# Leftover tokens of all batches in shared transfers, the guard's number in PSUM, the general path as a loop, and a new order of the work

## The chip, the cores and the metric

The kernel runs on one core of a Trainium2 chip. The metric is the device time of one execution in microseconds (us). Engines are named as the profile names them: PE (matrix products), PEld (weight loads of PE), DVE (vector), ACT (activation), POOL (GpSimd), SP (the engine whose queue issues every DMA of this kernel).

## The reference

Four batches of 12,480 tokens with 128 channels, 32 inducing vectors, and two weight matrices of a layer with 2,048 hidden units, all float32:

```python
def mab(q, kv):
    s = scale * (q @ kv.transpose(0, 2, 1))
    s = s - s.max(-1, keepdims=True)
    a = np.exp(s)
    a /= a.sum(-1, keepdims=True) + 1e-09
    return a @ kv
h = mab(I, x)              # 32 rows for each batch, from all its tokens
x = mab(x, h)              # every token, from those 32 rows
y = x @ w_in
g = y - np.tanh(y)
out = g @ w_out            # 49,920 x 128
```

## The kernel before

The kernel does not run the layer on 49,920 tokens. Every token's attention output is a mix of 32 rows of `h`, and these rows lie close together. So it expands `y - tanh(y)` around the mean row of each batch, carries the 32 rows through both weight matrices once for each batch (`linear`), and gets a 32 x 128 matrix `P`. An output token is then its 32 weights times `P`, divided by the sum of its weights. A guard (`bound`) works out how large the error of the expansion can be, against rounding and against the smallest sum of weights, and writes one number, `limit`. At the end all engines load `limit` and branch (L846, L847): if it is above zero, a general path computes the layer in full, token by token (`general`). With the inputs of this case the general path is not taken.

A batch is cut into 8 segments of 1,536 tokens and a rest of 192 (`NS`, `LEFT`), so there are nine steps for each batch, 36 in all. Each step occurs in two phases.

- `first(b)`: a segment is loaded with channels on the partitions (`xT`, L380), scored against the inducing vectors (`scores`, L357), copied to SBUF with its running maximum on DVE (L391). When the maxima of a group of segments are met, ACT takes the exponential (L461), DVE transposes blocks (L465), and PE accumulates the weighted sum of the tokens (L472). For that the tokens are needed with tokens on the partitions: 16 of the 32 segments are loaded a second time in that layout (`xn`, L455), the other 16 (`TURNED`) are transposed by PE (L447) and copied by ACT or DVE (L451).
- `second(b, s)`: the same `xT` tile is scored against `h` (L357 again), DVE finds a maximum (L625, L626), ACT takes the exponential (L629), PE multiplies by `P` (L636). DVE collects the sums of weights into `S_all` (L648) and takes reciprocals (L651). Each of the four quarters of a segment is then normalised in one of two ways: by DVE in one step (L660), or copied by ACT (L664) and multiplied by POOL (L669). The result is stored by SP (L695).

The rest of 192 tokens goes through the same steps with smaller tiles: `xr` (channels first, 98 KB, L380), `xnr` (tokens first, 98 KB, L455) and `otr` (output, 98 KB, L695), one transfer each for each batch, twelve in all. In SBUF `xr` has three places, `xnr` and `otr` two; scores of the rest stand on partitions 0 to 63.

Weights come in as 64-bit words (`weight`) and are turned into float32 by ACT, POOL and DVE over the first third of the span.

The order of the work is written out ahead by a planner in the program (`Plan.order`), not found at run time. Each operation is put in with an engine, an estimated cost, what it reads and writes, and a priority. The planner walks in simulated time over its own costs; whenever an engine is free it takes, of the ready operations, the one with the lowest priority number, with an added `STAY` for a change of PE mode. It also limits how many large buffers may hold tiles of a kind at one time (`MOST`). Priorities are built from the table `K`, one number for each kind of operation and batch; `DVQ` says how many quarters of a segment go to DVE at first, `GROUPS` where the maxima are met. Every engine then runs its list in that order, waiting on semaphores. SP's list holds all loads and stores, so a store whose data is not ready holds back what is behind it.

The guard's last steps run behind everything: `smin` is the minimum of all 432 columns of `S_all` (L750), PE turns it and two other columns into rows (L754 to L756), and `decide` makes `limit` on DVE in ten instructions (L763 to L771, with a scratch row `low` in SBUF):

```python
v.tensor_tensor(out=x[:, 3:4], in0=x[:, 3:4], in1=x[:, 3:4], op=ALU.mult)
v.tensor_tensor(out=x[:, 3:4], in0=x[:, 3:4], in1=x[:, 0:1], op=ALU.subtract)
v.tensor_scalar(out=limit, in0=x[:, 3:4], scalar1=0.0, scalar2=None, op0=ALU.max)
```

Of the kernel before, what the change touches and what calls it, by code (L numbers as in the profile page):

```python
# [26 lines left out]
SWITCH, STAY = 0.115, 73.1  # L27
MOST = dict(xT=15, xn=16, ot=61, pm=9)
K = dict(load=(-405.2, -73.6, 365.6, 732.0), step1=(189.5, 37.3, 86.1, 34.3), lag2=(-1344.7, 642.2, -187.9, 554.4),
         copy=(-966.7, 182.8, 582.0, 890.5), step2=(63.0, 5.9, 46.9, 4.9), turn=(3399.7, 2729.3, 3806.6, 3390.1), move=(-926.9,  # L30
         616.0, 643.2, -1883.0), nat=(445.7, -196.7, -60.7, 77.0), exp1=(-409.6, -1802.6, 1772.8, 577.3), et=(-1268.2, -670.6,
         821.4, -2142.2), acc=(63.5, 1115.9, -997.2, -2667.1), sc2=(498.0, -379.7, -952.9, 693.2), top=(984.0, 131.6, 1260.3,
         -21.4), exp2=(1257.9, -709.0, 2777.2, -857.8), prod=(-1778.1, 1760.3, -578.0, -21.4), rec=(-2172.0, -394.3, 355.7,
         404.0), ev=(2492.2, -544.6, -1227.1, -3030.9), off=(-545.7, 642.1, 1621.1, 2136.7), step3=(173.1, 138.3, 60.8, 306.6),
         st=(-962.2, -256.6, 745.9, -225.9), norm=(-114.8, 1199.2, -943.7, -185.5), lw1=-186.8, lw2=25.2, w1=74.7, w2=591.6,
         bound=2765.6)
# [3 lines left out]
LOADED = [(b, s) for b in range(4) for s in range(8) if s not in TURNED[b]]  # L40
WMIN = 1.125 * 2.0 ** -15
# [152 lines left out]
def fused_kernel(ctx, tc, xT, xn, xl, indT, w_in, w_out, out):  # L194
    nc = tc.nc
    C, NTOK = xT.shape
    B = xl.shape[0]
# [36 lines left out]
    PLACES = dict(big=23, xr=3, xnr=2, s1=11, et=3, ex=3, otr=2, mb=4, ps=8, W=1)  # L234
# [38 lines left out]
    sums_all = small("S_all", [128, B * COLS], 1)  # L273
# [85 lines left out]
    xT_b = {}  # L359

# [6 lines left out]
    def first(b, pri):  # L367
# [8 lines left out]
        for s in range(NSG):  # L376
            nq, sg, kb = shape(s)
            base = b * N + s * SG
            x = xT_b[b, s] = big("xT", [C, SG]) if s < NS else io_buf("xr", [C, LEFT])
            add("SP", 2.0 if s < NS else 0.35, lambda x=x, base=base, n=nq * sg: nc.sync.dma_start(out=x.get(), in_=xT[:, base:base + n]),  # L380
                writes=[x], pri=pri + s + K["load"][b])
            ps = misc()
            s1 = io_buf("s1", [128, SEG])
            add("PE", 0.645 if s < NS else 0.18, lambda x=x, ps=ps, nq=nq, sg=sg: scores(ps.get(), x.get(), nq, sg, indT_sb, True),
                reads=[x, ind_b, s1], writes=[ps], pri=pri + K["step1"][b] * s, mode="c")
            s1s.append(s1)
            part = Buf()
            mx_parts.append(part)

            def copy(ps=ps, s1=s1, s=s, P=nq * m, sg=sg):  # L390
                nc.vector.tensor_scalar(out=s1.get()[:P, :sg], in0=ps.get()[:P, :sg], scalar1=1.0, scalar2=None,  # L391
                                        op0=ALU.mult, op1=ALU.max, accum_out=mxg.get()[:P, s:s + 1])
            add("DVE", 0.52 if s < NS else 0.28, copy, reads=[ps, mxg], writes=[s1, part], pri=pri + K["step1"][b] * s + K["copy"][b])

# [34 lines left out]
        for s in range(NSG):  # L429
            nq, sg, kb = shape(s)  # L430
            P = nq * m
            g0 = group[s]
            q0 = p + K["step1"][b] * cut[g0 + 1] + K["step2"][b] * (s - cut[g0])
            if s < NS:
                x = big("xn", [128, KB, C])
            else:
                x = io_buf("xnr", [QL * 32, KL, C])
# [16 lines left out]
            else:  # L454
                add("SP", 2.0 if s < NS else 0.3, lambda x=x, s=s: nc.sync.dma_start(  # L455
                    out=x.get(), in_=xn[LOADED.index((b, s))] if s < NS else xl[b]), reads=[xT_b[b, s]], writes=[x], pri=q0 + K["nat"][b])
# [155 lines left out]
    def second(b, s, pri):  # L612
# [8 lines left out]
        add("PE", 0.645 if full else 0.18, lambda: scores(ps.get(), x.get(), nq, sg, hT_all[:, b, m:], True),  # L621
# [31 lines left out]
        ot = big("ot", [128, NQ * R, C]) if full else io_buf("otr", [SEGL, QL, C])  # L653
        pieces = []

        def slot(q0, q1):
            return ot.get()[:T, q0 * nr:q1 * nr, :]
# [34 lines left out]
        at = b * N + s * SG  # L692
        dst = out[at:at + nq * sg, :].rearrange("(p k) c -> p k c", p=T)
        for q0, q1 in ((0, 2), (2, 4)) if late and full else ((0, nq),):
            add("SP", (2.12 if full else 0.35) * (q1 - q0) / nq, lambda q0=q0, q1=q1: nc.sync.dma_start(  # L695
                out=dst[:, q0 * nr:q1 * nr, :], in_=slot(q0, q1)), reads=[ot, *pieces[q0:q1]], pri=pri + K["st"][b])


    def bound(pri):
# [41 lines left out]
        def least():  # L741
# [7 lines left out]
        smin, low = small("smin", [128, 1], 1), small("low", [1, 4], 1)  # L749
        add("DVE", 0.5, lambda: nc.vector.tensor_reduce(out=smin.get(), in_=sums_all.get(), axis=AX.X, op=ALU.min),  # L750
            reads=[sums_all, *s_parts], writes=[smin], pri=pri)

        def turn():
            nc.tensor.transpose(out=ps3.get()[:1, :B], in_=r1.get(), identity=ident[:B, :B])  # L754
            nc.tensor.transpose(out=ps3.get()[:1, 128:256], in_=r2.get(), identity=ident)
            nc.tensor.transpose(out=ps3.get()[:1, 256:384], in_=smin.get(), identity=ident)  # L756
        add("PE", 0.5, turn, reads=[r1, r2, smin, ident_b], writes=[ps3], pri=pri, mode="f")

        def decide():

            v = nc.vector
            x = low.get()
            v.tensor_reduce(out=x[:, 0:2], in_=ps3.get()[:1, 128:384].rearrange("o (k p) -> o k p", k=2), axis=AX.X, op=ALU.min)  # L763
            v.tensor_reduce(out=x[:, 2:3], in_=ps3.get()[:1, :B], axis=AX.X, op=ALU.min)
            v.tensor_tensor(out=x[:, 0:1], in0=x[:, 0:1], in1=x[:, 2:3], op=ALU.min)
            v.reciprocal(out=x[:, 2:3], in_=x[:, 1:2])
            v.tensor_scalar(out=x[:, 3:4], in0=x[:, 1:2], scalar1=-2.0, scalar2=2.0 * (m + SLACK), op0=ALU.mult, op1=ALU.add)
# [142 lines left out]
```

## Time and profile before

| | |
|---|---|
| Median of 3 runs | 187.9 us (186.53, 187.91, 187.90) |
| Profiled execution, its own time | 189.09 us |
| Its span, first to last instruction | 187.2 us |
| Busy: PE, PEld | 154.7 us (83%), 99.5 us (53%) |
| Busy: DVE, ACT, POOL | 149.6 (80%), 112.7 (60%), 95.5 (51%) |
| DMA | 68.84 MB, mean 368 GB/s |
| Mean granted clock of PE | 0.957 |

The profile is one execution on the chip. Busy time counts instructions that work, not those that wait, branch or issue transfers. An entry `L669 POOL TENSOR_TENSOR big<-big,mb 128x384` is line 669 of the kernel, engine, operation, written tile, read tiles, and partitions by elements. A table of stages has, after the length, the busy time of PE, PEld, DVE, ACT and POOL with the number of instructions in brackets, the granted PE clock as a share of full speed, the mean busy share of the 16 DMA engines, and the GB/s that they moved. A name with a q behind the engine (SPq) is the engine's sequencer, which waits, branches and issues transfers. A row of waits reads: who waited for whom, microseconds in total, times, longest. A row of one line's instructions has shortest, median and longest duration in ns and the first and last start in us. The chain of waits is the work that ended last, followed back from the end. The queue q1 carries the kernel's own transfers, q8 and q14 carry program code.

### The profile page before, as it was taken

What the parts mean: (1) busy time and instruction counts of PE and PEld (TensorE: products, weight loads), DVE (VectorE), ACT (ScalarE), POOL (GpSimd) and SP (SyncE); (2) the same over time, 40 slices, a digit from 0 to 9 for tenths busy, and PEclk for the clock granted to TensorE, in tenths of its full rate; (3) what the DMA queues carried; (4) which work ended last, traced back from release to release, by engine and by line L of the source; (5) the groups of instructions that cost most, each with busy time, mean ns of one, the idle gap of its engine ahead of it and who ended that gap; (6) DMA issues with size and microseconds to landing.
All of it is one profiled execution on the core that took longest, in us unless ns stands there. A gap on an engine that the chain in (4) does not pass through costs nothing.

```text
span 187.2 us, 7373 instructions
## 1 busy us (share of the span) xinstructions
PE 154.7 (83%) x2895; PEld 99.5 (53%) x2895; DVE 149.6 (80%) x574; ACT 112.7 (60%) x282; POOL 95.5 (51%) x114
## 2 busy tenths in 40 slices
PE   0799966879988999999999978999979988879500
PEld 0465554645345865565667864556556764646300
DVE  3268699999999987896889863599899879998950
ACT  3022389964168974756779953438589574578600
POOL 5000124672250368456755583460675886499960
PEclk9999999999999999999999995799999999999955
DMA  5999998999999999999999999699989999999991
GB/s 144 406 423 415 404 409 253 393 420 422 414 419 367 295 326 312 375 423 416 404 356 363 383 420 422 211 416 347 364 314 382 418 417 415 404 421 390 387 390 50
DMA packets 14489, 68.84 MB, mean 368 GB/s; under 512 B 1776, under 2 KB 2928, under 8 KB 14448
## 3 DMA queue, kind: packets, MB, share of 16 engines
q1 hardware_dynamic: 14448, 68.31, 94.2%
q8 instruction: 24, 0.39, 0.8%
q14 instruction: 17, 0.14, 0.2%
HBM read 42.75 MB, written 25.56 MB: 365 GB/s over the span
## 4 chain that ended last, share of the span: by engine, by line
PE 55%; DVE 20%; ACT 7%; DMA 6%; issue 5%; POOL 3%; SPq 0%; DVEq 0%; ACTq 0%; POOLq 0%
PE ps L357 17%; PE ps L636 13%; PE ps L447 10%; PE ps L472 9%; DMA big<-in_xn 3%; ACT s L461 3%; PE ps L353 3%; DMA big<-in_xT 2%; POOL big L669 2%; DVE s L391 2%; PE ps L527 2%; DVE mb L625 2%; DVE ps L327 2%; DVE big L320 2%; ACT big L323 1%
## 5 line engine op out<-in xcount | busy, mean ns | idle before, releaser
L669 POOL TENSOR_TENSOR big<-big,mb 128x384 f32<-128x384 f32 (+1 forms) x73 | 75.2, 1056 | 46.2 <-ACT big L664 41.9
L664 ACT COPY big<-ps 128x384 f32<-128x384 f32 x99 | 41.1, 488 | 8.2 <-DVE S_all L648 7.7
L636 PE MATMUL ps<-P_all,ex 32*128 32x129 f32 (+1 forms) x784 | 36.0, 294 | 4.1 <-issue 1.5
L636 PEld LDWEIGHTS ps<-P_all,ex 32*128 32x128 f32 (+1 forms) x784 | 28.1, 188 | 19.6 <-ACT big L664 5.2
L357 PE MATMUL ps<-big,indT_sb 128*32 128x384 f32 x256 | 28.1, 516 | 6.4 <-DMA big<-in_xT 6.0
L451 ACT COPY big<-ps 128x512 f32<-128x512 f32 x30 | 17.0, 587 | 25.8 <-PE ps L447 24.5
L472 PE MATMUL ps<-big,et 128*32 128x128 f32 x768 | 27.3, 275 | 5.8 <-DVE et L465 4.1
L629 ACT ACTIVATE ex<-ps,mb 128x384 f32<-128x384 f32 (+1 forms) x36 | 19.7, 553 | 17.8 <-DVE mb L626 10.8
L447 PEld LDWEIGHTS ps<-ident,big 128*128 128x128 f32 x192 | 21.6, 146 | 13.2 <-issue 4.9
L447 PE MATMUL ps<-ident,big 128*128 128x128 f32 x192 | 27.9, 290 | 0.9 <-DVE win_sb L329 0.9
L357 PE MATMUL ps<-big,hT_all 128*32 128x384 f32 x256 | 27.6, 502 | 0.2 <-DVE s L391 0.2
L472 PEld LDWEIGHTS ps<-big,et 128*32 128x32 f32 x768 | 21.0, 110 | 11.3 <-DVE et L465 5.0
L391 DVE TENSOR_SCALAR_CACHE_REDUCE s<-ps 128x384 f32<-128x384 f32 (+1 forms) x36 | 18.1, 513 | 8.8 <-PE ps L357 7.8
L461 ACT ACTIVATE s<-s,nbs 128x384 f32<-128x384 f32 (+1 forms) x36 | 21.0, 586 | 0.5 <-DVE nbs L412 0.5
L625 DVE TENSOR_REDUCE mb<-ps 128x1 f32<-128x384 f32 (+1 forms) x36 | 18.4, 511 | 2.6 <-PE ps L357 2.2
L648 DVE TENSOR_SCALAR S_all<-ps 128x3 f32<-128x3 f32 (+1 forms) x136 | 13.5, 153 | 7.3 <-PE ps L636 6.4
L465 DVE STREAM_TRANSPOSE et<-s 128x384 f32<-128x384 f32 (+1 forms) x36 | 18.1, 519 | 0.3
L660 DVE TENSOR_TENSOR big<-ps,mb 128x384 f32<-128x384 f32 x29 | 15.5, 544 | 0.3
L314 POOL TENSOR_SCALAR big<-big 128x512 f32<-128x512 f32 x8 | 5.4, 683 | 20.0 <-DMA big<-in_w_in 20.0
L451 DVE COPY big<-ps 128x512 f32<-128x512 f32 x18 | 12.3, 687 | 2.4 <-PE ps L447 2.2
L357 PEld LDWEIGHTS ps<-big,indT_sb 128*32 128x32 f32 x256 | 6.9, 113 | 12.0 <-issue 8.8
L357 PEld LDWEIGHTS ps<-big,hT_all 128*32 128x32 f32 x256 | 8.0, 111 | 5.1 <-issue 2.6
(118 smaller groups left out, 158.4 us busy)
## 6 DMA issues: line engine op xcount, KB each, us to landing
big<-in_xT SPq DMA_DIRECT2D x32, 768.0 KB, 8.8
out<-big SPq DMA_DIRECT2D x30, 768.0 KB, 7.6
big<-in_xn SPq DMA_DIRECT2D x16, 768.0 KB, 6.9
big<-in_w_in SPq DMA_DIRECT2D x4, 512.0 KB, 12.8
big<-in_w_out SPq DMA_DIRECT2D x4, 512.0 KB, 8.2
out<-big SPq DMA_DIRECT2D x4, 384.0 KB, 4.9
xr<-in_xT SPq DMA_DIRECT2D x4, 96.0 KB, 10.5
xnr<-in_xl SPq DMA_DIRECT2D x4, 96.0 KB, 7.0
```

The costliest lines, as they stand in the source:

```text
L357: nc.tensor.matmul(ps[q * m:(q + 1) * m, :sg], lhsT=w, rhs=seg(x, nq, None, q), start=True, stop=stop)
L391: nc.vector.tensor_scalar(out=s1.get()[:P, :sg], in0=ps.get()[:P, :sg], scalar1=1.0, scalar2=None, op0=ALU.mult, op1=ALU.max, accum_out=mx ...
L447: nc.tensor.transpose(out=ps.get()[:, k * 128:(k + 1) * 128], in_=xt.get()[:, c:c + 128], identity=ident)
L451: copy(x.get()[:, 4 * g:4 * g + 4, :].rearrange("p k c -> p (k c)"), ps.get())
L461: nc.scalar.activation(out=t, in_=t, func=AF.Exp, bias=nbs.get()[:P, g:g + 1], accum_out=sums.get()[:P, s:s + 1])
L465: add("DVE", 0.5 if s < NS else 0.25, lambda et=et, s1=s1s[s], P=P, sg=sg, kb=kb: nc.vector.transpose(out=et.get()[:P, :kb].rearrange("p k ...
L472: nc.tensor.matmul(hacc.get()[q * m:(q + 1) * m, g * C:(g + 1) * C], lhsT=et.get()[:P, k, :], rhs=x.get()[:P, k, :], start=first_k[g, q] = ...
L625: nc.vector.tensor_reduce(out=mb.get()[:P, 0:1], in_=ps.get()[:P, :sg], axis=AX.X, op=ALU.max)
L629: add("ACT", 0.49 if full else 0.28, lambda: nc.scalar.activation(out=ex.get()[:P, :sg], in_=ps.get()[:P, :sg], func=AF.Exp, bias=mb.get() ...
L636: nc.tensor.matmul(o_b[q].get()[:T, r * (C + 1):(r + 1) * (C + 1)], lhsT=ex.get()[p, r * T:(r + 1) * T], rhs=P_all[p, b, :], start=True, s ...
L664: nc.scalar.copy(out=slot(q, q + 1), in_=o(q)[:, :, :C])
L669: nc.gpsimd.tensor_tensor(out=x, in0=x, in1=mb.get()[:T, 2 + q0 * nr:2 + q1 * nr].unsqueeze(2).to_broadcast([T, w, C]), op=ALU.mult)
```

## The change

1. The rests of all four batches are loaded by two transfers: `xr` (128 partitions x 3,072 bytes) for the channels-first layout, and `xl` for the other one, where batches 0 and 2 lie on partitions 0 to 63 and batches 1 and 3 on 64 to 127. Both are issued with batch 0. Scores of the rest of odd batches therefore stand on partitions 64 to 127 (`at`). Rests get scratch tiles of their own (`s1r`, two places; `s1` has ten places in place of eleven).
2. The rests are stored by two transfers: batches 0 to 2 together once batch 2's rest is normalised, then batch 3.
3. The guard takes the minimum of `S_all` in two parts: all columns but those of the last three steps first (an early instruction), then the last 36 columns and the early result. Two of the three turns and their reductions (`room`) move ahead of the last step. What is left (`decide`) is five instructions on a scratch row in PSUM, with a formula that needs no reciprocal.
4. In the general path the loop over the 16 blocks of hidden units becomes a loop of the program (`tc.For_i`) in place of 16 copies of its body; partial outputs are added by DVE in SBUF and no longer accumulated in PSUM.
5. `K`, `STAY`, `MOST`, `TURNED`, `GROUPS` and `DVQ` have new values. 16 segments are turned and 16 loaded twice, as before.

```diff
-SWITCH, STAY = 0.115, 73.1
-MOST = dict(xT=15, xn=16, ot=61, pm=9)
+SWITCH, STAY = 0.115, 31.6
+MOST = dict(xT=15, xn=12, ot=48, pm=7)
 ...
-TURNED = ((0, 1, 2, 3, 4, 5, 6, 7), (1, 2, 6), (1, 2, 4, 7), (0,))
-GROUPS = ((0,), (0,), (0,), (0, 3))
-DVQ = ((2, 1, 1, 1, 2, 3, 2, 0, 1), (2, 1, 0, 2, 1, 3, 1, 2, 1), (2, 2, 0, 1, 2, 1, 1, 3, 1), (2, 1, 2, 3, 1, 2, 3, 2, 0))
+TURNED = ((0, 1, 2, 3, 4, 5, 6, 7), (0, 1, 2, 4), (2, 4, 7), (0,))
+GROUPS = ((0,), (0,), (0,), (0, 4))
+DVQ = ((2, 0, 3, 2, 2, 3, 2, 2, 1), (2, 2, 2, 2, 2, 1, 1, 1, 1), (1, 2, 1, 1, 2, 0, 2, 2, 1), (3, 1, 1, 0, 1, 2, 2, 3, 0))
 ...
-    PLACES = dict(big=23, xr=3, xnr=2, s1=11, et=3, ex=3, otr=2, mb=4, ps=8, W=1)
+    PLACES = dict(big=23, s1=10, s1r=2, et=3, ex=3, mb=4, ps=8, W=1)
 ...
+    rest = small("xr", [C, B, LEFT], 1)
+    rest_n = small("xnr", [128, B // 2, KL, C], 1)
+    rest_o = small("otr", [SEGL, B, QL, C], 1)
+    rest_pieces = []
 ...
+            elif b == 0:
+                add("SP", 1.0, lambda: nc.sync.dma_start(out=rest.get(), in_=xr), writes=[rest], pri=pri + s + K["load"][b])
+            at = 0 if s < NS else QL * m * (b % 2)
 ...
+            elif b == 0:
+                add("SP", 1.0, lambda: nc.sync.dma_start(out=rest_n.get(), in_=xl), reads=[rest], writes=[rest_n], pri=q0 + K["nat"][b])
 ...
+        rest_pieces.extend(pieces)
+        if b < B - 2:
+            return
+        b0 = 0 if b == B - 2 else b
+        dst = out.rearrange("(b n) c -> b n c", b=B)[b0:b + 1, NS * SG:, :].rearrange("b (p q) c -> p b q c", p=T)
+        add("SP", 0.35 * (b + 1 - b0), lambda: nc.sync.dma_start(out=dst, in_=rest_o.get()[:, b0:b + 1]),
+            reads=[rest_o, *rest_pieces], pri=pri + K["st"][b])
+        rest_pieces.clear()
 ...
-        add("DVE", 0.5, lambda: nc.vector.tensor_reduce(out=smin.get(), in_=sums_all.get(), axis=AX.X, op=ALU.min),
-            reads=[sums_all, *s_parts], writes=[smin], pri=pri)
+        n1 = B * COLS - KB
+        n2 = n1 - 2 * KB
+        early = Buf()
+        add("DVE", 0.5, lambda: nc.vector.tensor_reduce(out=sums_all.get()[:, B * COLS:], in_=sums_all.get()[:, :n2], axis=AX.X, op=ALU.min),
+            reads=[sums_all, *s_parts[:-3]], writes=[early], pri=pri)
+        add("DVE", 0.15, lambda: nc.vector.tensor_reduce(out=smin.get(), in_=sums_all.get()[:, n2:], axis=AX.X, op=ALU.min),
+            reads=[sums_all, early, *s_parts[-3:]], writes=[smin], pri=pri)
 ...
+        def room():
+            v = nc.vector
+            v.tensor_reduce(out=c0.get()[:, 0:1], in_=ps3.get()[:1, 128:256], axis=AX.X, op=ALU.min)
+            v.tensor_reduce(out=c0.get()[:, 1:2], in_=ps3.get()[:1, :B], axis=AX.X, op=ALU.min)
+            v.tensor_reduce(out=c0.get()[:, 0:1], in_=c0.get(), axis=AX.X, op=ALU.min)
+        add("DVE", 0.3, room, reads=[ps3], writes=[c0], pri=pri)
 ...
         def decide():
 ...
-            v.reciprocal(out=x[:, 2:3], in_=x[:, 1:2])
 ...
+            x = ps4.get()[:1, 256:259]
+            v.tensor_reduce(out=x[:, 0:1], in_=ps4.get()[:1, :128], axis=AX.X, op=ALU.min)
+            v.tensor_scalar(out=x[:, 1:2], in0=x[:, 0:1], scalar1=-2.0, scalar2=2.0 * (m + SLACK), op0=ALU.mult, op1=ALU.add)
+            v.tensor_scalar(out=x[:, 2:3], in0=x[:, 0:1], scalar1=c0.get()[:, 0:1], scalar2=x[:, 0:1], op0=ALU.mult, op1=ALU.mult)
+            v.tensor_scalar(out=x[:, 1:2], in0=x[:, 1:2], scalar1=x[:, 1:2], scalar2=x[:, 2:3], op0=ALU.mult, op1=ALU.subtract)
+            v.tensor_scalar(out=limit, in0=x[:, 1:2], scalar1=0.0, scalar2=None, op0=ALU.max)
+        add("DVE", 0.7, decide, reads=[ps4, c0], writes=[ps4], pri=pri, lag=2.5)
 ...
-            for f in range(NF):
+            with tc.For_i(0, NF) as f:
```

More of the change, by code (lines that the diff above doesn't have):

```diff
@@ L193, in fused_kernel @@
 @with_exitstack
-def fused_kernel(ctx, tc, xT, xn, xl, indT, w_in, w_out, out):
+def fused_kernel(ctx, tc, xT, xn, xr, xl, indT, w_in, w_out, out):
     nc = tc.nc
     C, NTOK = xT.shape
-    B = xl.shape[0]
+    B = xr.shape[1]
     m = indT.shape[1]
@@ L652, in second @@
             reads=[part], writes=[mb, part2], pri=pri + K["rec"][b])
[L653 removed]
+        ot = big("ot", [128, NQ * R, C]) if full else rest_o
         pieces = []
         def slot(q0, q1):
[L657 removed]
+            return ot.get()[:T, q0 * nr:q1 * nr, :] if full else ot.get()[:, b, q0:q1, :]
         def whole(q):
@@ L691, in second @@
                 needed=lambda x=done[q0]: x.eng == "ACT")
[L692 to L696, printed above, removed]
+        if full:
+            at = b * N + s * SG
+            dst = out[at:at + nq * sg, :].rearrange("(p k) c -> p k c", p=T)
+            for q0, q1 in ((0, 2), (2, 4)) if late else ((0, nq),):
+                add("SP", 2.12 * (q1 - q0) / nq, lambda q0=q0, q1=q1: nc.sync.dma_start(
+                    out=dst[:, q0 * nr:q1 * nr, :], in_=slot(q0, q1)), reads=[ot, *pieces[q0:q1]], pri=pri + K["st"][b])
+            return
+        rest_pieces.extend(pieces)
+        if b < B - 2:
+            return
+        b0 = 0 if b == B - 2 else b
[3 more added lines that the diff above has]
+        rest_pieces.clear()
     def bound(pri):
@@ L757, in bound @@
-        add("PE", 0.5, turn, reads=[r1, r2, smin, ident_b], writes=[ps3], pri=pri, mode="f")
+        smin = small("smin", [128, 1], 1)
+        n1 = B * COLS - KB
[5 more added lines that the diff above has]
+            reads=[sums_all, early, *s_parts[-3:]], writes=[smin], pri=pri)
@@ L759, in decide @@
+        add("DVE", 0.3, room, reads=[ps3], writes=[c0], pri=pri)
+        ps4 = misc()
+        add("PE", 0.3, lambda: nc.tensor.transpose(out=ps4.get()[:1, :128], in_=smin.get(), identity=ident),
+            reads=[smin, ident_b], writes=[ps4], pri=pri, mode="f")
         def decide():
             v = nc.vector
-            x = low.get()
-            v.tensor_reduce(out=x[:, 0:2], in_=ps3.get()[:1, 128:384].rearrange("o (k p) -> o k p", k=2), axis=AX.X, op=ALU.min)
-            v.tensor_reduce(out=x[:, 2:3], in_=ps3.get()[:1, :B], axis=AX.X, op=ALU.min)
@@ L771, in decide @@
-            v.tensor_scalar(out=limit, in0=x[:, 3:4], scalar1=0.0, scalar2=None, op0=ALU.max)
-        add("DVE", 0.9, decide, reads=[ps3], writes=[low], pri=pri)
+            x = ps4.get()[:1, 256:259]
+            v.tensor_reduce(out=x[:, 0:1], in_=ps4.get()[:1, :128], axis=AX.X, op=ALU.min)
+            v.tensor_scalar(out=x[:, 1:2], in0=x[:, 0:1], scalar1=-2.0, scalar2=2.0 * (m + SLACK), op0=ALU.mult, op1=ALU.add)
+            v.tensor_scalar(out=x[:, 2:3], in0=x[:, 0:1], scalar1=c0.get()[:, 0:1], scalar2=x[:, 0:1], op0=ALU.mult, op1=ALU.mult)
@@ L858, in fused_kernel @@
                 general(gen, bi, bi * N + NS * SG, QL, SEGL, KL, 1)
-_INS = ["xT", "xn", "xl", "indT", "w_in", "w_out"]
+_INS = ["xT", "xn", "xr", "xl", "indT", "w_in", "w_out"]
 def kernel(**inputs):
```

91 lines of the change are left out of this document (49 added, 42 removed).

## The prediction

> **What bounds the kernel now.** I read the page first (span, busy shares, chain), then the busy time by stage, then the end of the span instruction by instruction, then the chain of waits around the one stage where the TensorE clock fell.
>
> ```profile
> span 187.2 us, 7373 instructions
> PE 55%; DVE 20%; ACT 7%; DMA 6%; issue 5%; POOL 3%; SPq 0%; DVEq 0%; ACTq 0%; POOLq 0%
> ...
> 24.00:37.00 13.00, 8.79 (x217) 7.19 (x219) 12.68 (x33) 12.41 (x31) 5.42 (x8) 1.00 0.95 349
> 37.00:59.00 22.00, 18.79 (x294) 9.48 (x286) 21.41 (x68) 11.72 (x27) 8.89 (x8) 1.00 1.02 417
> 59.00:96.00 37.00, 36.62 (x747) 23.57 (x747) 30.70 (x128) 26.07 (x63) 21.22 (x20) 1.00 0.99 363
> 112.00:121.00 9.00, 8.09 (x124) 4.07 (x128) 3.51 (x19) 3.07 (x9) 4.31 (x5) 0.62 0.86 323
> 121.00:141.00 20.00, 18.77 (x377) 11.82 (x372) 18.81 (x85) 13.64 (x39) 9.81 (x9) 1.00 0.96 360
> 141.00:160.00 19.00, 17.00 (x428) 11.75 (x424) 16.29 (x79) 12.64 (x36) 13.33 (x14) 1.00 1.01 407
> 160.00:175.00 15.00, 12.88 (x246) 8.56 (x239) 13.27 (x64) 11.26 (x28) 12.91 (x13) 1.00 1.00 403
> 182.00:187.20 5.20, 0.00 (x0) 0.00 (x0) 0.00 (x0) 0.00 (x0) 0.00 (x0) 0.50 0.26 80
> ```
>
> No single engine is the limit. The stages read (columns after the length: PE, weight load, DVE, ACT, POOL, clock, DMA share, GB/s): DVE and ACT fill 24 to 37, DVE alone 37 to 59 (21.41 of 22), PE 59 to 96 (36.62 of 37), and from 141 to 175 the DMA engines are full (1.01, 1.00) while PE, DVE and POOL each run at 85 to 90%. After 182 no engine computes at all: 5.2 us of the span are tail. The tail in detail:
>
> ```profile
> 175.59 4.76 POOL L669 TENSOR_TENSOR big<-big,mb 128x384 f32<-128x384 f32 x6
> 175.59 0.57 DVE L750 TENSOR_REDUCE smin<-S_all 128x1 f32<-128x432 f32 x1
> ...
> 176.62 0.39 DVE L763 TENSOR_REDUCE low<-ps 1x2 f32<-1x256 f32 x1
> ...
> 178.82 0.75 DVE L769 TENSOR_TENSOR low<-low 1x1 f32<-1x1 f32 x1
> ...
> 180.39 0.14 DVE L771 TENSOR_SCALAR limit<-low 1x1 f32<-1x1 f32 x1
> 180.94 0.33 SPq L695 DMA_DIRECT2D out<-otr  x1
> out<-otr SPq DMA_DIRECT2D x1, 96.0 KB, 4.6
> L847 PEldq COMPARE_BRANCH  x1: 4033/4033/4033, 181.4 to 181.4; - x1
> L847 ACTq EVENT_SEMAPHORE  x1: 17/17/17, 181.8 to 181.8; - x1
> L847 DVEq EVENT_SEMAPHORE  x1: 21/21/21, 186.1 to 186.1; - x1
> SPq L906 <- DVEq L847: 1.9, 1, 1.9
> ```
>
> Two things race to the end. One is the last store: POOL runs its pieces without a break until it is issued at 180.94, and it lands 4.6 us later, at 185.5. The other is the guard: L771 writes `limit` at 180.53, every engine but SP has loaded it by 181.4 (where the branch row starts) and jumps past the general path. ACT comes out of that branch at 181.8, PE spends 4.03 us in it, DVE comes out at 186.1. SP waits 1.9 us for DVE alone. From 186.1 to 187.2 is the closing barrier. So the guard ends last, by 186.1 - 185.5 = 0.6 us.
>
> **The change, part by part.** *Guard.* The final minimum covers 37 columns in place of 432. A reduction of 128x1 from such a short row costs about what L771 costs, 0.15 against 0.57 us. The decision falls from ten DVE instructions to five, on PSUM, and none of the five is a TENSOR_TENSOR of one element in SBUF, the kind of row that stands at 0.75. Five at 0.14 to 0.39 with gaps of 0.1 make about 1.3 us, against 180.53 - 176.62 = 3.9 now. `limit` is then written some 0.4 + 2.6 = 3 us earlier, near 177.5. If the branch still took PE 4 us and DVE 4.6 after its load, they would come out near 183, ahead of 185.5. That slow row is as long as one POOL piece (4.76 / 6 = 0.79 us), and POOL runs without a break beside it, which is what an exclusive resource would give. [...] Were it instead the dependence of one tiny instruction on the next that costs 0.75, five of them would take 3.8 us, nothing would be gained by this edit, and the next one would have to carry the term.
>
> *General path as a loop.* It is never executed here. The unrolled body has some 17 DVE instructions for each of 16 blocks in each of two calls, over 540; PE some 200; ACT two for each block, about 75, and ACT came out of the branch 0.4 us after 181.4. With the loop the DVE and PE bodies are each shorter than ACT's is now, so their branch should cost what ACT's costs. Either of these two edits alone takes the guard off the end. Next late is the store: 185.5 + 1.1 for the barrier = 186.6 in place of 187.2. Gain 0.6 us, and no more, whatever the guard saves. Beyond nothing on the other side: a guard moved earlier cannot delay a store that POOL sets.
>
> *The moved minimum and `room`.* The long minimum (0.57), two transposes and three small reductions (about 0.5) go ahead of the last normalisations on DVE. DVE has 15 - 13.27 = 1.7 us free in 160 to 175 and POOL sets the end, so I take nothing; without that cover it is 1.1 us.
>
> *Transfers.*
>
> ```profile
> 56.15 1.11 SPq L455 DMA_DIRECT2D xnr<-in_xl  x2
> ...
> 121.16 0.51 SPq L380 DMA_DIRECT2D xr<-in_xT  x1
> ...
> 141.11 0.48 SPq L455 DMA_DIRECT2D xnr<-in_xl  x1
> q1 hardware_dynamic: 108, 0.10, 65.8%
> ```
>
> The same bytes move. Four of the twelve small loads (xr of batch 3, xnr of batches 1 to 3), 4 x 98 KB = 393 KB, go from later stages to the first 30 us. At 417 GB/s that is 0.94 us of DMA time taken out of stages where the DMA share stands at about 1. It is put in ahead of 24 to 37, where the share is 0.95 (0.65 us free), so most is covered; the remaining 0.3 us is a rival's price. Small packets also cost more: in 182.5 to 183, almost only 1 KB store packets, 0.10 MB took 65.8% of 0.5 us = 0.33 us, against 0.24 at 417 GB/s, an estimate of 0.09 us for each small transfer. The packets of the eight loads become two to four times longer; four of these lay in full stages: 0.35 us. The stores keep their 1 KB packets, and the three that become one wait for batch 2; the last one, batch 3, stays 96 KB and alone. SP issues ten transfers fewer; its queue has 0% of the chain, so nothing. DMA term: 0.94 + 0.35 = 1.3, between 0 (if compute, at 85 to 90%, sets those stages) and 1.3; I take all of it because 141 to 175 runs at a share of 1.0, and keep 0 for the range.
>
> *New order.* Priorities, turned segments (16 before and after), store limits: work and bytes stay the same, so no row prices it. Its bounds come from the costliest accident of the present order:
>
> ```profile
> 111.37 1.55 issue
> ...
> 116.06 1.86 PE ps L527 x16
> 150.56 1.07 PE ps L527 x16
> 113.00:119.70 6.70, 6.70 (x60) 2.80 (x64) 2.50 (x13) 2.33 (x7) 3.26 (x4) 0.50 0.83 337
> q8 instruction: 1, 0.02, 5.5%
> ```
>
> PE stands for 1.55 us on nothing but "issue", in the middle of one group of products, right after a code block was fetched (the one q8 packet of 110.4 to 111.4). Then the granted clock is 0.50 for 6.7 us, and the sixteen products of L527 take 1.86 us where those of batch 3 take 1.07. At half clock 6.7 us of work lose 3.35 us; with the stall 4.9 us on the chain. A new order can lose this or meet it twice: -4.9 to +4.9 us. With no row on either side I take 0.
>
> Sum against the profiled execution: 189.09 us (span 187.2 + 1.9 around it) - 0.6 - 1.3 = 187.2. The median of the runs shown is 187.9, 1.2 below that execution, so the forecast is 187.9 - 1.9 = 186.0.
>
> **Rivals.** *A, the accident goes.* For it: code blocks are fetched all along the span and only this fetch is followed by a stop, so its place depends on what the DMA queue holds when PE runs fast. What is gained at 112 must be used before 141, since the stores after it fill the DMA engines: free DMA time there is 9 x 0.14 + 20 x 0.04 = 2.1 us. So 186.0 - 2.1 = 183.9, and 181.1 if all 4.9 came through.
>
> *B, a second accident; slower.* One mechanism: PE runs out of fetched instructions and the clock halves. Place: 59 to 96, where PE has 0.4 us free in 37. It decides once a code block arrives later than PE empties the one it has and the pause touches the clock's decision, as 1.55 us did here. Price 4.9: 186.0 + 4.9 = 190.9; the pause alone gives 187.5. Against: the other fetches cost nothing that the chain shows. [...] This trace shows 0.50 behind a pause of 1.55, so the measurement keeps 4.9.
>
> *C, the early loads cost what the late ones gave.* w_in and w_out come behind 393 KB more in a stage that ACT and DVE fill to 95%; 0.3 us is uncovered and the DMA term is 0 because compute sets 141 to 175. Then 187.9 - 0.6 + 0.3 = 187.6. The same comes out if the guard still ends last and only the DMA term is real (186.6).
>
> **Chances.** Forecast 0.45, with its own range 184.8 to 187.3 (DMA term 0 to 1.3, order within 1.2); A 0.24; B 0.18; C 0.13. About 1% (1.9 us) can be told from no change, so "faster" is below 186.0: half of the forecast's share and A, 0.47. "Slower" is above 189.8: most of B and a little from an order that is simply worse, 0.20. Within: 0.33. The range 182.8 to 189.6 takes in A except its extreme, C, the forecast and B's pause without the clock; it leaves out 0.2.
>
> **What would show it.** Right: DVE's decision rows near 1.3 us with none above 0.4; PE's branch row of some 50 ns; SP's last wait is for the DMA of the last store, not for DVE; from the last store's issue to the end 5.7 us in place of 6.3; the two leftover loads stand in the first 30 us and no small load after. Wrong: PE or DVE still 4 us in the branch and still last; a granted clock below 1 in another place, with an "issue" pause ahead of it; the last POOL piece later than 181, which would mean that the new order and not the tail decides.

## The result and the profile after

Of 20 executions each, the changed kernel has a median of 190.6 us and the kernel before 190.5. The comparison goes by undisturbed executions, of which before has fewer but quicker ones (down to 186.5, against 188.6): there the ratio is **1.0119, with a 95% interval from 1.0076 to 1.0162**, so by this comparison the change is slower by 1.2%, while by the medians of all executions the two are alike. Two repeats gave 1.0101 [1.0004, 1.0197] and 1.0058 [1.0011, 1.0105]. The forecast was 186.0 us, faster by 1%, counted from 187.9, the median of the first three of before's executions.

The profile shown here is that of the last repeat, an execution of 190.8 us. Its page, the span and the chain's shares by engine:

```profile
span 188.3 us, 7349 instructions
PE 51%; DMA 20%; DVE 16%; issue 4%; ACT 3%; POOL 2%; POOLq 1%; SPq 0%; DVEq 0%; ACTq 0%
```

The time lies 190.8 - 188.3 = 2.5 us above the span; before it was 1.9. And DMA has 20% of the chain, against 6%. The busy time by stage, same columns as in the prediction:

```profile
24.00:37.00 13.00, 9.34 (x191) 7.10 (x192) 12.53 (x32) 11.49 (x30) 5.30 (x6) 1.00 0.86 317
37.00:59.00 22.00, 17.18 (x283) 10.55 (x274) 19.88 (x58) 10.96 (x22) 9.74 (x9) 1.00 0.98 386
112.00:121.00 9.00, 7.63 (x196) 5.77 (x194) 6.19 (x34) 4.20 (x13) 6.72 (x8) 1.00 1.02 419
```

The clock at 112 to 121 is 1.00 where it was 0.62, but in the two other profiles of the changed kernel it is 0.83 and 0.81 there. And the DMA engines are idle 14% of 24 to 37 (before 5%), and DVE, which filled 37 to 59 with 21.41 us, has 19.88. The groups of the guard, with busy time and mean ns of one:

```profile
L806 DVE TENSOR_SCALAR ps<-ps 1x1 f32<-1x1 f32 x1 | 0.3, 283 | 0.0
L805 DVE TENSOR_SCALAR ps<-ps,bt_c 1x1 f32<-1x1 f32 x1 | 0.3, 277 | 0.0
L803 DVE TENSOR_REDUCE ps<-ps 1x1 f32<-1x128 f32 x1 | 0.3, 275 | 0.0
L804 DVE TENSOR_SCALAR ps<-ps 1x1 f32<-1x1 f32 x1 | 0.2, 153 | 0.0
L807 DVE TENSOR_SCALAR limit<-ps 1x1 f32<-1x1 f32 x1 | 0.1, 145 | 0.0
L781 DVE TENSOR_REDUCE smin<-S_all 128x1 f32<-128x37 f32 x1 | 0.1, 132 | 0.0
```

The five decision rows take 1.13 us together, the last minimum 0.13: as forecast. The branch, instruction by instruction (duration min/median/max in ns, first and last start in us):

```profile
L888 SPq EVENT_SEMAPHORE  x4: 17/17/17, 186.7 to 187.0; - x4
...
L888 PEldq COMPARE_BRANCH  x1: 358/358/358, 180.8 to 180.8; - x1
...
L888 DVEq EVENT_SEMAPHORE  x1: 21/21/21, 181.4 to 181.4; - x1
L888 SPq COMPARE_BRANCH  x1: 45/45/45, 183.7 to 183.7; - x1
```

PE spends 0.36 us in the branch, not the 50 ns that the prediction named but no longer 4 us, and DVE is out at 181.4: the guard is off the end, as forecast. But **SP** branches at 183.7 and executes its next instruction at 186.7. The list of waits of SP, and the DMA queues between 183.7 and 186.7 (packets, MB, share):

```profile
SPq L888 <- SPq L888: 3.0, 1, 3.0
```

```profile
q14 instruction: 1, 0.01, 0.8%
```

SP waits 3.0 us for nothing but itself, and one packet of code is fetched in that time. That SP waits for this packet is a reading; the row doesn't say whose code it is. In the kernel before, SP branched at 182.2 and went on at 182.7:

```profile
L847 SPq EVENT_SEMAPHORE  x4: 17/17/17, 182.7 to 183.0; - x4
...
L847 SPq COMPARE_BRANCH  x1: 50/50/50, 182.2 to 182.2; - x1
```

### The profile page after: what moved, and what is told of

Its sections match the earlier page's. It is cut to its first block, busy times and chain, and to the rows that moved or that the text cites. A ratio compares the mean times of both kernels' runs of the same rounds, so it can differ in the third digit from the quotient of the medians.

```text
span 190.9 us, 7349 instructions
## 1 busy us (share of the span) xinstructions
PE 156.4 (82%) x2895; PEld 102.0 (53%) x2895; DVE 148.8 (78%) x573; ACT 112.9 (59%) x283; POOL 93.7 (49%) x111
## 4 chain that ended last, share of the span: by engine, by line
PE 55%; DVE 17%; DMA 14%; issue 5%; ACT 2%; POOL 2%; POOLq 1%; SPq 0%; DVEq 0%; ACTq 0%
PE ps L358 17%; DMA big<-in_xT 14%; PE ps L652 14%; PE ps L488 11%; PE ps L460 8%; DVE mb L641 3%; PE ps L354 2%; PE ps L543 2%; POOL big L685 2%; DVE big L321 2%; DVE s L403 1%; DVE big L464 1%; DVE S_all L664 1%; DVE nbs L424 1%; DVE top L420 1%
## 5 line engine op out<-in xcount | busy, mean ns | idle before, releaser
L685 POOL TENSOR_TENSOR big<-big,mb 128x768 f32<-128x768 f32 (+1 forms) x70 | 73.3, 1075 | 47.7 <-ACT big L680 38.6
L680 ACT COPY big<-ps 128x384 f32<-128x384 f32 x97 | 40.5, 492 | 10.3 <-DVE S_all L664 6.3
L652 PE MATMUL ps<-P_all,ex 32*128 32x129 f32 (+1 forms) x784 | 37.2, 290 | 3.1 <-DVE P_all L615 1.6
L652 PEld LDWEIGHTS ps<-P_all,ex 32*128 32x128 f32 (+1 forms) x784 | 29.7, 185 | 14.5 <-ACT ex L645 3.7
L358 PE MATMUL ps<-big,indT_sb 128*32 128x384 f32 x256 | 28.8, 525 | 10.4 <-DMA big<-in_xT 8.6
L488 PE MATMUL ps<-big,et 128*32 128x128 f32 x768 | 27.3, 275 | 5.5 <-DVE et L480 3.4
L488 PEld LDWEIGHTS ps<-big,et 128*32 128x32 f32 x768 | 21.1, 110 | 10.4 <-DVE et L480 5.2
L403 DVE TENSOR_SCALAR_CACHE_REDUCE s<-ps 128x384 f32<-128x384 f32 x32 | 17.4, 548 | 10.2 <-PE ps L358 9.9
L476 ACT ACTIVATE s<-s,nbs 128x384 f32<-128x384 f32 x32 | 19.7, 620 | 3.3 <-DVE nbs L424 3.3
L480 DVE STREAM_TRANSPOSE et<-s 128x384 f32<-128x384 f32 x32 | 17.5, 561 | 1.6 <-ACT s L476 1.0
L676 DVE TENSOR_TENSOR big<-ps,mb 128x384 f32<-128x384 f32 x31 | 16.7, 545 | 0.4
L464 DVE COPY big<-ps 128x512 f32<-128x512 f32 x18 | 12.3, 690 | 2.2 <-PE ps L460 2.0
```

What stands on the lines that cost most here:

```text
L358: nc.tensor.matmul(ps[q * m:(q + 1) * m, :sg], lhsT=w, rhs=seg(x, nq, None, q), start=True, stop=stop)
L403: nc.vector.tensor_scalar(out=s1.get()[p, :sg], in0=ps.get()[p, :sg], scalar1=1.0, scalar2=None, op0=ALU.mult, op1=ALU.max, accum_out=mxg. ...
L464: copy(x.get()[:, 4 * g:4 * g + 4, :].rearrange("p k c -> p (k c)"), ps.get())
L480: add("DVE", 0.5 if s < NS else 0.25, lambda et=et, s1=s1s[s], P=P, sg=sg, kb=kb: nc.vector.transpose(out=et.get()[P, :kb].rearrange("p k ...
L652: nc.tensor.matmul(o_b[q].get()[:T, r * (C + 1):(r + 1) * (C + 1)], lhsT=ex.get()[p, r * T:(r + 1) * T], rhs=P_all[p, b, :], start=True, s ...
L680: nc.scalar.copy(out=slot(q, q + 1), in_=o(q)[:, :, :C])
```

## The experiments

All ratios are to the kernel before, run beside each on the same chip. "Around" is the mean of time minus span. "SP" is the time from SP's branch to its next instruction, "PE" the PE branch row, both in the profiled execution. Rows are lines of the compiled program, equal neighbours taken together. For e7 there is no ratio; before's median beside it was 190.49.

| run | what it is | executions | median us | ratio [95%] | around us | SP us | PE us |
|---|---|---|---|---|---|---|---|
| e1_loop_only | before + loop | 6 | 191.85 | 1.0156 [1.0085, 1.0227] | 2.39 | 2.9 | 0.24 |
| e2_after_unrolled | changed, no loop | 12 | 190.25 | 0.9968 [0.9912, 1.0025] | 1.91 | 0.5 | 6.36 |
| e3_parts_pinned | all parts, old order | 6 | 191.99 | 1.0113 [1.0022, 1.0204] | 2.09 | 2.6 | 0.24 |
| e4_after_again | changed, repeat | 6 | 192.0 | 1.0101 [1.0004, 1.0197] | 2.41 | 2.9 | 0.36 |
| e5_f_outer | before, one short loop | 12 | 190.74 | 1.0068 [0.9992, 1.0144] | 1.80 | 0.5 | 3.39 |
| e6_sp_long | before, longer SP code | 6 | 190.97 | 1.0102 [1.0020, 1.0183] | 2.05 | 4.4 | 3.83 |
| e7_after_f_outer | changed, short SP code | 12 | 189.88 | - | 1.81 | 0.5 | 5.02 |
| e8_rests | before + shared transfers | 12 | 190.13 | 1.0028 [0.9976, 1.0079] | 1.90 | 0.5 | 4.23 |
| e9_one_loop | before + flat loop | 12 | 189.62 | 0.9962 [0.9887, 1.0036] | 1.80 | 0.5 | 0.35 |
| e10_after_one_loop | changed, flat loop | 12 | 190.04 | 1.0054 [1.0008, 1.0101] | 1.85 | 0.5 | 0.35 |
| e11_new_order | before + new constants | 6 | 207.99 | 1.0896 [1.0769, 1.1024] | 1.79 | 0.5 | 3.77 |
| e12_old_order | changed, old constants | 6 | 201.91 | 1.0683 [1.0605, 1.0762] | 2.00 | 2.6 | 0.36 |
| e13_parts_one_loop | all parts, old order, flat loop | 12 | 189.32 | 1.0042 [0.9989, 1.0095] | 1.79 | 0.5 | 0.24 |
| e14_one_loop_again | e9 again | 12 | 188.34 | 0.9931 [0.9873, 0.9990] | 1.82 | 0.5 | 0.36 |
| e15_after_third | changed, repeat | 12 | 190.95 | 1.0058 [1.0011, 1.0105] | 2.35 | 3.0 | 0.36 |

### Which part loses: e1, e2, e3, e4

The theory: the loop loses, through SP's branch. Rivals: the new order's stages, or the parts. e1 is the kernel before with the diff's hunk for the general path alone; e2 is the changed kernel without that hunk:

```diff
-            for f in range(NF):
+            with tc.For_i(0, NF) as f:
```

> The kernel before with one edit: the loop in the general path. The order of the executed work does not change. If the forecast's tail is right (the guard ends last by 0.6 us because PE and DVE fetch code in the branch), PE's branch falls from 4.03 us below 0.5, DVE is out of it near 182 in the trace's time, and the ratio to the kernel before is 0.997. Rival, read off the trace of the changed kernel: SP's own branch gets the code fetch (2.9 us there). Here SP branches at about 182.2, so it would come out near 185.1, just under the landing of the last store at 185.5: ratio 0.997 to 1.002, and SP waiting on itself and not on DVE.

> The changed kernel with the general path unrolled as before; the order of the executed work is that of the changed kernel. If SP's 2.9 us in the branch are a price of the loop, SP comes out half a microsecond after it enters, the last store (landing at 189.1 in the trace) ends the span, and this kernel is 0.8 us faster than the changed one (ratio between them 0.996). If the loop is what spared PE and DVE, they come out 4.1 to 4.6 us after the branch, near 188, still ahead of that store: no loss. If the stall at SP has another cause, such as where SP stands in its code, the two kernels are equal within 0.2 us.

e3 has all parts of the change in the order of before, written out operation by operation; e4 is the changed kernel unedited.

> All parts of the change but the new order: rests in two loads and two stores, the guard on PSUM with its minimum in two parts, the loop; the planner still plans the twelve transfers, so every other instruction stands where it stands in the kernel before. By the forecast's sum: -0.6 (tail) -1.3 (transfers) = -1.9 us, ratio 0.990. If the transfers gain nothing because compute sets the late stages: -0.6, ratio 0.997. If loading the rests early is what made the change slow: +0.3 us or more, ratio 1.002 to 1.012. If the new order alone made it slow, this kernel is at 0.990 to 0.997 while the changed kernel on the same chip stands near 1.012.

> The changed kernel itself, unedited, beside the three others on one chip: ratio 1.008 to 1.016 if what was measured holds on this chip.

The loop alone, every operation ahead of it as before, gives 1.0156. Everything but the loop gives 0.9968, not to be told from nothing. e3, with all parts and the loop in the old order, gives 1.0113, beside 1.0101 for the changed kernel: the loss doesn't need the new order. The branch of e1:

```profile
L852 SPq EVENT_SEMAPHORE  x4: 17/17/17, 185.8 to 186.1; - x4
...
L852 PEldq COMPARE_BRANCH  x1: 241/241/241, 181.9 to 181.9; - x1
...
L852 DVEq EVENT_SEMAPHORE  x1: 21/21/21, 182.4 to 182.4; - x1
L852 SPq COMPARE_BRANCH  x1: 45/45/45, 182.9 to 182.9; - x1
```

The loop does what the prediction said, PE and DVE are out by 182.4, and what it hadn't, SP from 182.9 to 185.8. The rows show a smaller loss than 1.0156 would be: from the last store's issue to the end it is 187.5 - 181.2 = 6.3 us as before, and around the span lie 2.36 to 2.40 us in each of e1's six executions, against 1.73 to 1.91 in each of 98 of before, 0.6 us more. The medians of all executions differ by 1.0 us (191.85 against 190.84). What the rest of the 1.0156 is stays open. In e2 the two have changed places:

```profile
L883 SPq EVENT_SEMAPHORE  x4: 17/17/17, 185.0 to 185.2; - x4
...
L883 PEldq COMPARE_BRANCH  x1: 6363/6363/6363, 181.7 to 181.7; - x1
...
L883 SPq COMPARE_BRANCH  x1: 45/45/45, 184.5 to 184.5; - x1
```

In these two either PE and DVE wait or SP does; PE's 6.36 us is more than the 4.1 to 4.6 that I had expected. What e1 doesn't say is why a loop in which SP has no work should delay SP.

### Why SP waits: e5, e6, e9

A loop is run by every engine, so two nested loops in each of two calls put compares, branches and semaphore waits into SP's code as well: 148 rows, against 136 before. Theory: it is the length of each engine's own code behind the branch. e5 turns the loops around, so that SP has one loop for each call, as before (136 rows), and PE and DVE have short code:

```diff
-        with tc.For_i(0, nq) as qi:
-            with tc.For_i(0, NF) as f:
+        with tc.For_i(0, NF) as f:
+            for qi in range(nq):
```

e6 leaves the blocks written out and lengthens SP's code with a loop of one turn (148 rows):

```diff
         with tc.For_i(0, nq) as qi:
-            for f in range(NF):
+            with tc.For_i(0, 1):
+                for f in range(NF):
```

> The kernel before with a general path that loops over f outside and writes the segments q out inside, so that PE and DVE have short code there (some 70 and 160 rows in place of 130 and 570) while SP's code has the same rows as before (one loop for each of the two calls). Theory (it is SP's code length that costs, because SP's jump falls past what is loaded): SP comes out of its branch 0.5 to 0.6 us after it, the time around the span is 1.8 to 1.9 us as before, PE is out by 182, and the ratio to the kernel before is 0.993 to 1.002. Rival (a loop in the general path costs by itself, wherever it stands): SP 2.6 to 2.9 us, 2.4 us around the span, ratio 1.008 to 1.02, as with the two nested loops. DVE may still wait for code; it would then be out by 185.5 to 186.1 and the ratio would be at 1.000.

> The kernel before, its blocks f still written out, with one loop of a single turn put around them: SP's code becomes as long as in the loop version (148 rows against 136), PE's and DVE's stay long. Theory (SP's code length): SP's branch takes 2.6 to 2.9 us and 2.3 to 2.4 us lie around the span in place of 1.8 to 1.9; DVE's own branch (out at 186.1) covers SP's within the span, so the time grows by 0.5 to 1.2 us: ratio 1.002 to 1.008. Rival (the loop over f itself): SP 0.5 us, 1.8 to 1.9 us around the span, ratio 0.998 to 1.002.

The branch of e5, then of e6:

```profile
L852 SPq EVENT_SEMAPHORE  x4: 17/17/17, 183.7 to 183.9; - x4
...
L852 PEldq COMPARE_BRANCH  x1: 3393/3393/3393, 183.2 to 183.2; - x1
...
L852 SPq COMPARE_BRANCH  x1: 50/50/50, 183.2 to 183.2; - x1
...
L852 DVEq EVENT_SEMAPHORE  x1: 21/21/21, 187.3 to 187.3; - x1
```

```profile
L848 SPq EVENT_SEMAPHORE  x4: 17/17/17, 186.5 to 186.7; - x4
...
L848 SPq COMPARE_BRANCH  x1: 45/45/45, 182.1 to 182.1; - x1
L848 ACTq EVENT_SEMAPHORE  x1: 17/17/17, 185.2 to 185.2; - x1
...
L848 DVEq EVENT_SEMAPHORE  x1: 21/21/21, 186.1 to 186.1; - x1
```

SP follows its own code length in both: 0.5 us with a loop, 4.4 us without the loop over f. The time around the span follows it too, 1.80 and 2.05. My numbers missed several times. e6's SP took 4.4 and not 2.9, so DVE didn't cover it, and the ratio is 1.0102 in place of 1.002 to 1.008; the time around the span rose to 2.05 only, not to 2.3; ACT, with the same extra loop, waited as well; and e5's PE, with little more code than with the nested loops, took 3.4 us again. So e5 saves nothing at the end, and its ratio, 1.0068 and between the two expectations, says nothing for or against. PE's row doesn't grow in proportion to the length. Counted in single instructions of the compiled programs, PE has 6,049 in e9, 6,103 in e1, 6,117 in e5 and 6,433 before, and its branch row takes 0.35, 0.24, 3.39 and 4.03 us, with a step between 6,103 and 6,117. Nor does SP's wait follow the length: its code is equally long in e1 and in e6, with 2.9 and 4.4 us.

e9 is a single loop over all pairs, with which no engine's code is long (SP 136 rows, PE 642, DVE 577):

```diff
-        with tc.For_i(0, nq) as qi:
-            with tc.For_i(0, NF) as f:
+        with tc.For_i(0, nq * NF) as i:
+            qi, f = i // NF, i % NF
```

> The kernel before with the general path as one loop over all pairs of q and f in each call: SP's code has the rows of before (136) and PE and DVE have few (642 and 577 rows in all, against 726 and 1075 before). Theory (the length of each engine's code behind the branch, SP's too, sets the wait): PE, DVE and SP all come out within 0.7 us of the branch, the last wait is for the DMA of the last store, 1.8 us lie around the span, and the span ends with the store: from its issue to the end 5.7 us in place of 6.3. That is the prediction's 0.6 us: ratio 0.994 to 1.000 where the rest of the span is alike. Rival (a loop costs something elsewhere too): 2.1 to 2.4 us around the span or a wait of 2.6 us on some engine, ratio 1.003 to 1.015.

> The kernel before with the single loop again, for a narrower interval. Theory: 0.993 to 1.000, the prediction's 0.6 us of tail. Rival (the earlier 0.996 was the spread between executions): above 1.002.

e9's branch, and SP's list of waits:

```profile
L853 SPq EVENT_SEMAPHORE  x4: 17/17/17, 183.8 to 184.1; - x4
...
L853 PEldq COMPARE_BRANCH  x1: 350/350/350, 183.3 to 183.3; - x1
...
L853 SPq COMPARE_BRANCH  x1: 50/50/50, 183.3 to 183.3; - x1
...
L853 DVEq EVENT_SEMAPHORE  x1: 21/21/21, 183.9 to 183.9; - x1
```

```profile
SPq L912 <- DMA out<-otr: 1.1, 1, 1.1
```

All engines are out within 0.6 us and SP's last wait is for the last store, as the prediction wanted it for the changed kernel. From the store's issue to the end it is 5.95 us in e9 and 5.5 in e14, against 6.3 before. By its ratio e9 can't be told from before; e14, the same kernel, is faster at 0.9931 [0.9873, 0.9990]. This edit by itself has the lowest median in the table.

### What SP's wait costs the changed kernel: e7, e10

e7 and e10 are the changed kernel with the loops of e5 and of e9.

> The changed kernel with f outside and q written out inside, so that SP's code in the general path has as few rows as before the change. Theory (SP's code length is what the change loses by): SP is out 0.5 to 0.6 us after its branch, the last wait is for the last store's DMA, 1.9 us lie around the span in place of 2.4, and the time falls by 0.5 to 2.5 us against the changed kernel: ratio to the kernel before 0.990 to 1.003. Rival (the change loses in its stages, by the new order or the early loads): ratio 1.008 to 1.012 as unedited, although SP's branch is short.

> The changed kernel with that single loop in its general path. Theory: SP's 2.9 us in the branch and 0.5 us around the span go; the time is 0.6 to 1.5 us below the changed kernel's, a median of 189.0 to 190.4, and what is left against the kernel before is the stages' alone: ratio 0.995 to 1.004. Rival (SP's wait was covered, the stages set the change's time): as the changed kernel, 190.5 to 192 and 1.010.

> The changed kernel unedited beside these two, on the same chip. Theory: 2.4 us around the span, ratio 1.006 to 1.013. Rival (its loss is only in how the undisturbed executions are picked): 0.998 to 1.004.

In e7 SP is out after 0.5 us and 1.81 us lie around the span, as expected, and PE waits 5.0 us instead. Its median of 189.88 stands beside before's 190.49. The end of e10, and the same row in e15, the changed kernel:

```profile
182.22 0.35 SPq L720 DMA_DIRECT2D out<-otr  x1
```

```profile
182.42 0.35 SPq L720 DMA_DIRECT2D out<-otr  x1
```

From there to the end of the span it is 187.2 - 182.2 = 5.0 us in e10, and 188.3 - 182.4 = 5.9 in e15. With the time around the span (1.85 against 2.35) SP's code costs 0.9 + 0.5 = 1.4 us by these two profiles. The medians, on different chips, differ by 0.9 (190.95 against 190.04). The store's own landing, 4.0 us in e15, hides most of the 3.0 us. This is one pair: among kernels in which no engine waits in the branch, issue to end goes from 5.0 us (e10) to 6.4 (e13), with the store landing after 4.0 to 5.4. e10 stays at 1.0054 [1.0008, 1.0101], so something else seems to be left.

### The transfers and the order: e8, e11, e12, e13

> The kernel before with the leftover tokens alone loaded by two transfers and stored by two; guard, general path and the plan's order as before. The prediction's DMA term: 1.3 us less, ratio 0.993, and DMA idle time between 96 and 175 us at most that of before (2.2 us). Rival (compute sets those stages, or the early loads give it back): ratio 0.998 to 1.003.

e8 has the shared transfers alone. It gains nothing, 1.0028. Its chain early on, and then the same two places of before (start, us, what):

```profile
34.53 5.85 DMA big<-in_xT
...
60.53 1.31 PE ps L483 x48
```

```profile
33.80 1.59 ACT s L461 x6
...
59.40 1.31 PE ps L472 x48
```

With the leftover loads ahead, the chain runs through a segment's load at 34.5, where before it ran through ACT's exponential, and the same 48 products start 1.1 us later, at 60.5. The start varies by itself: in the six profiles of the old order with the old transfers (before, e1, e5, e6, e9, e14) it lies at 58.8 to 60.0, in the three with the shared ones (e3, e8, e13) at 59.6 to 60.5, about 1 us later in the mean. This is the way of rival C, at three times its 0.3 us. That the early loads cause it is argued from the chains of e8 and e13, in which the load stands; it isn't in that of e3. Between 60 and the end e8's profiled execution is the shorter one: its span is 186.2 us, and its clock stays at 1.00 from 112 to 121. So the late gain may be there, and the ratio says only that the sum is near nothing.

e11 is the kernel before with the new order's constants (these, and K, GROUPS, DVQ); e12 the changed kernel with the old ones.

```diff
-SWITCH, STAY = 0.115, 73.1
-MOST = dict(xT=15, xn=16, ot=61, pm=9)
+SWITCH, STAY = 0.115, 31.6
+MOST = dict(xT=15, xn=12, ot=48, pm=7)
```

> The kernel before with the changed kernel's priorities, limits, groups and DVE queues (its turned segments stay); transfers, guard and general path as before. From the executions so far: in the old order the granted clock has a mean of 0.964 (45 executions of before), in the new order 0.974 (after, 20), and at an equal clock the new order's span is about 0.7 us longer. Theory (the order changes both, one up, one down): mean clock 0.971 to 0.977, 1.8 us around the span, median 189.5 to 190.7, ratio 0.998 to 1.008. Rival (the parts, not the order, moved the clock and the span): clock 0.962 to 0.967 and a span like before's.

> The changed kernel with the old priorities, turned segments, groups and DVE queues (one limit, pm, stays at 7). Theory: mean clock 0.961 to 0.967 as before, SP's branch 2.6 to 2.9 us and 2.1 to 2.4 us around the span, median 190.5 to 192, ratio 1.003 to 1.012. Rival (the parts moved the clock): 0.972 or more.

Both miss by far, 1.09 and 1.07. They don't price the order: the constants were found for one set of operations, and with another set the planner makes another order from them. I had treated the two as separable.

> The kernel before with the change's transfers and its guard on PSUM at the old order, and the general path as one loop with short SP code. Theory (of the change's 1.2%, SP's code is 0.3 to 0.5%, the parts are nothing, and the new order's waits for early loads are the rest): the guard is off the end, 1.8 to 1.9 us lie around the span, and the ratio is 0.992 to 1.000, so at or below the kernel before. Rival (the parts themselves cost what the order was blamed for): ratio 1.004 to 1.012 although SP is out of its branch in 0.6 us.

e13 has all parts, the old order and e9's loop: 1.0042, across both bounds of what was expected; its median of 189.3 stands beside before's 191.1. It doesn't settle whether the parts cost up to 1%; they don't gain anything beside e14 (188.3).

What the new order does is read from its chain (e15; start, us, what) and from SP's waits between 18 and 52 us:

```profile
38.40 13.02 DMA big<-in_xT
...
98.14 8.01 DMA out<-big
106.22 11.29 DMA big<-in_xT
```

```profile
SPq L389 <- PE ps L488: 10.5, 3, 9.5
```

A segment's load lands at 38.4 + 13.0 = 51.4 and the chain runs through it. Ahead of that SP's queue stands for 9.5 us, since the next load needs a buffer that the products of L488 haven't freed. At 98 to 117 a load waits until a store has left its buffer. None of these pieces is in the chain of before. The load at 37 to 39, with 12.3 to 13.5 us, is in the chain of all six profiles of the new order (SP's wait is 8.3 to 9.7 us there) and in none of the old; the pieces from 98 on are in e15 alone. To price this the executions are taken at one granted clock, those with a mean of 0.97 or more over the span:

| SP's code | order | kernels | executions at 0.97 or more, of all | mean of these, us |
|---|---|---|---|---|
| short | old | before, e5, e8, e9, e13, e14 | 56 of 157 | 189.2 (standard error 0.2) |
| long | old | e1, e3, e6 | 6 of 18 | 191.2 (0.5) |
| short | new | e2, e7, e10 | 30 of 36 | 189.9 (0.2) |
| long | new | changed, e4, e15 | 32 of 38 | 190.7 (0.2) |

(One execution of before, at 204.3 us, is left out.) At the same clock the new order costs 189.9 - 189.2 = 0.7 us and SP's code 190.7 - 189.9 = 0.8 us on top. Together 1.5 us, 0.8%, which lies in the intervals of the changed kernel's three ratios. The groups hold kernels with different parts, from different chips, and in the old order SP's code comes to 191.2 - 189.2 = 2.0 us from six executions, so the split is an estimate. That SP's code is one cause was shown one edit at a time.

## Why the prediction was wrong

**The step that failed** is in "General path as a loop": "Gain 0.6 us, and no more" and "Beyond nothing on the other side: a guard moved earlier cannot delay a store that POOL sets." I had counted the instructions of PE, DVE and ACT in the body and concluded that "their branch should cost what ACT's costs". SP was left out because it has next to no work in the body. But a loop's own instructions are in every engine's code, in SP's 148 rows against 136. In e1 PE's row fell from 4.03 us to 0.24 and DVE was out at 182.4 in place of 186.1, but SP took 2.9 us in place of 0.5, and 3.0 in e15. By the rows of e10 and e15 it costs 0.9 us in the span and 0.5 around it, where the sum had -0.6. With the loop written so that SP's code stays short, the term comes: 0.3 and 0.7 us by the rows of e9 and e14, and 0.9962 and 0.9931 (0.7 and 1.3 us) by the ratios, against 0.6 forecast.

The time was also missed by its base. The 187.9 that the sum starts from was the median of three executions; over 20 of the same kernel it is 190.5. Of the 4.6 us between 186.0 and 190.6, 2.6 are this, and 2.0 are the sum's -1.9, of which nothing came.

That a skipped branch can wait was in the trace of before: PE's 4.03 us row. I took this for a cost of the body's length and didn't ask what sets it. The runs show a step for two engines: PE's row is 0.24 us in e1 and 3.39 in e5, with 14 instructions more, and SP's wait is 0.5 us at 136 rows in e9 and 2.9 at 148 in e1. What happens in that time no row shows. The question for every engine, SP too, would have been how much code lies behind its branch.

**Guard: right.** 1.13 us against "about 1.3", no row above 0.4. With POOL busy beside it, the old form still has its row of 0.75 in e9 (the group is L769 there too); in PSUM nothing is above 0.28. So it was not the dependence. An exclusive resource would fit (0.75 us beside POOL's pieces of 0.79), but no run has the old form without POOL beside it. `limit` came earlier by 0.9 us only (180.5 to 179.6) and not by 3: the last minimum stands right behind the last sums and reciprocals, at 177.7. Nothing hung on it.

**Store next late: right** where SP is out of the way: 5.0 us from issue to end in e10, 5.5 in e14, 5.95 in e9 (181.85 to 187.8), against 5.7 forecast; 6.4 in e13, whose store lands late.

**Transfers: wrong, -1.3 forecast and about 0 measured.** "I take all of it because 141 to 175 runs at a share of 1.0" took the relief at its full price and the 0.3 us of cover missing before 37 us as another rival's. e8 measured 1.0028 [0.9976, 1.0079], with a start about 1 us later near 60 us. Two slips carried no term: SP issues eight transfers fewer (four for twelve), not ten, and the 186.6 given as "the same" as rival C's 187.6 is another time.

**New order: the value of 0 was not far off, its reasoning was.** The bounds were made from one accident. In fact two things moved against each other: the mean granted clock rose (rival A, in part), and loads came onto the chain, which no step of the prediction had. The sign that I had named for this, a last POOL piece later than 181, is there: it runs from 181.8 to 182.4 in e15, against 180.3 to 180.9 before. The accident itself is not gone from the new order. The chain of the changed kernel's first profile, and that of e7, which has the same order (start, us, what):

```profile
114.11 1.70 issue
```

```profile
74.08 1.35 issue
```

Behind the first the clock is 0.50 from 117.9 to 121.3. The second is rival B as it was written, a pause in the stage 59 to 96: the fifteen products behind it take 2.79 us, against 1.49 in e4, and the clock over 75 to 96 is 0.92, against 1.00. A pause of that length alone doesn't do it: in before PE stood for 1.66 us ahead of 27.9, waiting for DVE, and in the changed kernel's first profile for 2.12 us ahead of 29.5, and behind both the clock stayed at 1.00 up to 37. That PE had run out of code in the pauses with a fall behind them was my reading; the rows say only "issue".

## What to carry to other kernels

Code that is never executed had a price here at the branch that skips it, engine by engine and in a step: PE's row went from 0.24 to 3.39 us between 6,103 and 6,117 instructions, SP's wait from 0.5 to 2.9 us between 136 and 148 rows. Count the instructions that loops, barriers and waits add on the engines that have no work there, SP above all. A nest of loops flattened to one kept all of them short here (0.35 us for PE and 0.5 for SP in e9). A number in a hand-made order belongs to one set of operations: price it from waits and buffers in the trace, and not from the worst accident of the old order.

## What was not expected of the hardware

SP's long code also shows outside the span: the time around it is 2.0 to 2.4 us with it and 1.8 to 1.9 without, in the old order (2.39 in e1, 2.05 in e6, 2.09 in e3) as in the new (2.35 to 2.41). A further packet of code is fetched after the end of the span, 0.3 us after it in before and in e9, 1.6 us in e1 and 2.3 in the changed kernel (at 190.6 in e15, whose span ends at 188.3), and none is recorded in e6 and e10; what asks for it, and why later, is not shown.

The granted clock differs between executions of one kernel. Over 97 executions of before the mean is 0.964: 30 below 0.96 take 192.1 us on average, 37 from 0.96 to 0.97 take 190.6, and 30 from 0.97 on take 189.4. The new order reaches 0.97 in 62 of 74 executions, the old one in 62 of 175. Which feature of the order does that was not tested. It would give back in most executions what the change loses at an equal clock, which fits the two medians being alike.
